# A planner that frees buffers later, first means from tiles already loaded, and pairs of attention tiles in one bank

## The chip, the cores and the metric

The kernel runs on one core of a Trainium2 chip. The metric is device microseconds of one execution, from the median of several runs. Before the change it is 660.25 us (three runs, 660.16 to 660.63). The engines are PE (TensorE: matmuls, with weight loads shown as PEld), ACT (ScalarE), DVE (VectorE), POOL (GpSimd) and SP, which only issues the DMAs here.

## What is computed

Three steps in float32, on q, k, v of 2 x 8 x 768 x 64 (batch, heads, tokens, head size):

```
k_sum = max of k over blocks of 32 tokens;  v_sum = mean of v over blocks of 32 tokens
scores = [ q k^T / 8 where |i - j| < 16, else -1e9 ;  q k_sum^T / 8 + log 32 ]
x = softmax(scores) [ v ; v_sum ]                         # 24 blocks beside the window
x = x / rms(x) * g;  x = (silu(x Wg) * (x Wv)) Wo         # 512 -> 1536 -> 512
out = elu(x Win) Wout                                     # 512 -> 2048 -> 512, 1536 tokens
```

The weights come in as 64-bit floats and are turned into 32-bit ones on the chip.

## The kernel before, in words

**Tiles and stages.** The attention works on 24 tiles of 64 tokens (12 for each batch), all heads of a tile together. A tile needs a copy of the keys of its window and of the 24 block maxima (`copy_keys`), a `scores` group, the softmax on DVE, ACT and POOL, a transpose of the weights (`turn_e`, copied out by `copy_e` to a buffer `ats`) and `apply_v`, 8 matmuls whose outputs are 64 partitions high and which multiply them with the values in one of four buffers `va0` to `va3`: 96 rows of v, loaded for this tile by `load_v`, and below them 24 rows of block means. `copy_x` brings the result into `xT`, the input of the networks for 512 tokens.

The block means are made on PE: `load_vtok` brings 256 tokens of v at a time, 2 tokens to a partition, `mean_v` multiplies them with the constant `blocks` in sets of four matmuls, each 32 partitions high, three calls of two sets for each batch. `place_v` and `repeat_v` put the means into the four `va` buffers.

Tokens are then taken in three blocks of 512. The first network runs in 12 chunks of 128 hidden features per block (`project` twice, gate, `down`), the second in 16 chunks per block: `project` into a PSUM bank `ph`, `elu_a` (exponential, ACT), `elu_b` and `elu_c` (DVE; `elu_c` is the last that reads `ph`), `act_a` and `act_b` that split the result into a high and a low part, and `down`. Both parts of weights and inputs are multiplied, three matmuls of 512 columns for each product. The two parts of a weight are made by `split_a` (a cast, ACT) and `split_b` (a subtraction, DVE) into one of four buffers of the pool `ws`. The attention of the second and third block is woven into the first network of the block before.

**What sets the order.** The class `Order` holds every operation with its engines, its cost in us, a due time, and what it reads and writes. `issue` (L74) plays a schedule forward: an engine that is free takes, of the operations that are ready and for which buffers are free, the one with the least due time; the instructions are then written out in the order in which they were taken, so each engine's order is fixed, and on the chip semaphores alone decide when each starts. A result is ready for another engine 0.2 us after PE's end and 0.13 after any other's (`hop`, L71). A buffer goes back to its pool when the last operation that uses it is popped from a heap of events (L176, L188 to L195). A heap entry is (time, number, kind); entries that only wake the planner, for an operation becoming ready, carry the number -1. `pick` (L124) gives a new tile the first free one of the tags that it may have; for `ph` these are the four banks m0, m1, t0, t1. The due times are written in the `add_...` functions and moved by the table `SHIFT`, by operation and by stretch of due time (`EDGES`). The queue of SP is planned in the same way, and it is the order of the DMAs.

## Time and profile before

| what | value |
|---|---|
| median of the runs | 660.25 us |
| the profiled execution's own time | 660.16 us |
| its span, first to last instruction | 658.0 us |
| PE busy | 644.2 us, 98% |
| DVE / ACT / POOL busy | 455.3 / 360.9 / 70.4 us |
| DMA: bytes moved | 53.42 MB |

Times below are from the start of the span. A busy share counts an engine as busy as long as one of its instructions runs; matmuls overlap, so their starts, not their durations, tell how fast PE goes. In a row of the timeline the number after the start is from the first start to the last end of the merged group, and xN is how many instructions it holds; a float32 matmul of the attention is recorded as two.

### The profile page before, as it was taken

The page shows a single profiled execution, that of the slowest core. Times are in us where ns is not written, and L with a number is a line of the kernel's source. Part 1 is how long each engine was busy: PE and PEld are TensorE (multiplying, and loading weights), DVE is VectorE, ACT ScalarE, POOL GpSimd, SP SyncE. Part 2 cuts the span into 40 slices and gives each one's busy share as a digit, 9 for nine tenths or more (in the row PEclk, how much of TensorE's full clock was granted, in tenths as well). Part 3 has the DMA queues.
Part 4 walks back from the last instruction along what each step waited for, and adds up shares of the span by engine and source line. Part 5 has one row for each costly group of instructions (what it writes and reads, how often), then busy time and mean ns, then how long its engine had stood idle before and what let it go on. Part 6 is the DMA issues. An engine that isn't in the chain of part 4 may idle for free.

```text
span 658.0 us, 9324 instructions
## 1 busy us (share of the span) xinstructions
PE 644.2 (98%) x3424; PEld 525.1 (80%) x3424; DVE 455.3 (69%) x842; ACT 360.9 (55%) x805; POOL 70.4 (11%) x130
## 2 busy tenths in 40 slices
PE   6999998999999999999999999999999999999997
PEld 4888887887888888888888888887787777877776
DVE  6789778857745557489999984655665555755554
ACT  4889768775766664355555553444444334534441
POOL 5741133233000030000000000000000000000000
PEclk9999999999999999999999999999999999999999
DMA  9986995721003000015565300000010000100001
GB/s 224 251 200 197 294 290 170 233 75 45 13 21 130 0 1 1 0 33 188 177 190 185 125 0 1 0 1 0 1 65 0 1 0 1 64 1 1 0 1 64
DMA packets 76957, 53.42 MB, mean 81 GB/s; under 512 B 45168, under 2 KB 71792, under 8 KB 76912
## 3 DMA queue, kind: packets, MB, share of 16 engines
q1 hardware_dynamic: 76912, 52.83, 28.6%
q8 instruction: 27, 0.44, 0.3%
q14 instruction: 18, 0.15, 0.1%
HBM read 49.68 MB, written 3.15 MB: 80 GB/s over the span
## 4 chain that ended last, share of the span: by engine, by line
PE 90%; DVE 4%; ACT 3%; POOL 1%; DMA 1%; SPq 1%; issue 1%; ACTq 0%; POOLq 0%
PE acc L888 34%; PE ph L820 21%; PE pg L820 14%; PE s L613 2%; PE pv L663 2%; PE pv_3c L820 1%; PE pv_7c L820 1%; PE pv_8c L820 1%; PE pv_2c L820 1%; PE pv_11c L820 1%; PE pv_6c L820 1%; PE pv_9c L820 1%; PE at L652 1%; PE pv_1c L820 1%; PE pv_10c L820 1%; PE pv_4c L820 1%
## 5 line engine op out<-in xcount | busy, mean ns | idle before, releaser
L820 PE MATMUL ph<-xb,ws_i 128*128 128x512 f32 x576 | 141.7, 394 | 0.0
L888 PE MATMUL acc<-ws_p,act 128*128 128x512 f32 x576 | 138.3, 389 | 0.0
L820 PEld LDWEIGHTS ph<-xb,ws_i 128*128 128x128 f32 x576 | 105.9, 188 | 30.3 <-issue 9.0
L888 PEld LDWEIGHTS acc<-ws_p,act 128*128 128x128 f32 x576 | 108.1, 188 | 22.5
L888 PE MATMUL acc<-act,ws_o 128*128 128x512 f32 x432 | 107.7, 394 | 0.0
L820 PE MATMUL pg<-x,ws_g 128*128 128x512 f32 (+1 forms) x432 | 105.7, 389 | 0.0
L888 PEld LDWEIGHTS acc<-act,ws_o 128*128 128x128 f32 x432 | 79.8, 188 | 16.6 <-issue 0.2
L820 PEld LDWEIGHTS pg<-x,ws_g 128*128 128x128 f32 x432 | 78.1, 188 | 15.9 <-issue 0.2
L299 DVE TENSOR_TENSOR ws_p<-raw_p,ws_p 128x512 fp32r<-128x512 f32 x48 | 33.2, 691 | 74.1 <-ACT ws_p L288 74.1
L288 ACT CAST ws_p<-raw_p 128x512 fp32r<-128x512 f32 x48 | 29.8, 622 | 89.9 <-PE ph L820 87.8
L288 ACT CAST act<-ex 128x512 fp32r<-128x512 f32 x48 | 29.7, 619 | 49.6 <-DVE ex L868 49.6
L875 DVE TENSOR_TENSOR act<-ex,act 128x512 fp32r<-128x512 f32 x48 | 33.2, 692 | 25.1 <-ACT act L288 24.4
L299 DVE TENSOR_TENSOR ws_g<-raw_g,ws_g 128x512 fp32r<-128x512 f32 x35 | 24.6, 704 | 19.0 <-ACT ws_g L288 18.9
L299 DVE TENSOR_TENSOR ws_i<-raw_i,ws_i 128x512 fp32r<-128x512 f32 x48 | 32.9, 685 | 6.9 <-ACT ws_i L288 6.9
L288 ACT CAST ws_i<-raw_i 128x512 fp32r<-128x512 f32 x48 | 29.8, 620 | 13.9 <-PE ph L820 8.3
L288 ACT CAST ws_o<-raw_o 128x512 fp32r<-128x512 f32 x36 | 22.3, 619 | 23.1 <-PE pg L820 7.8
L868 DVE SCALAR_TENSOR_TENSOR ex<-ph,ex 128x512 f32<-128x512 f32 x48 | 33.1, 690 | 1.4
L288 ACT CAST ws_g<-raw_g 128x512 fp32r<-128x512 f32 x35 | 21.6, 617 | 20.4 <-PE pg L820 13.8
L288 ACT CAST ws_v<-raw_v 128x512 fp32r<-128x512 f32 x35 | 21.7, 619 | 20.2 <-PE acc L888 7.4
L853 DVE SCALAR_TENSOR_TENSOR th<-th,pg 128x512 f32<-128x512 f32 x36 | 24.6, 684 | 6.6 <-ACT th L849 6.4
L860 ACT ACTIVATE ex<-ph 128x512 f32<-128x512 f32 x48 | 28.5, 594 | 0.0
L875 DVE TENSOR_TENSOR act<-th,act 128x512 fp32r<-128x512 f32 x36 | 25.1, 696 | 4.7 <-ACT act L288 4.4
(209 smaller groups left out, 947.7 us busy)
## 6 DMA issues: line engine op xcount, KB each, us to landing
st_i<-in_moe_w_in SPq DMA_DIRECT2D x16, 512.0 KB, 3.8
st_p<-in_moe_w_out SPq DMA_DIRECT2D x16, 512.0 KB, 3.3
st_g<-in_moe_w_gate SPq DMA_DIRECT2D x12, 512.0 KB, 5.2
st_v<-in_moe_w_val SPq DMA_DIRECT2D x12, 512.0 KB, 5.1
st_o<-in_moe_w_out SPq DMA_DIRECT2D x12, 512.0 KB, 4.5
va<-in_v SPq DMA_DIRECT2D x20, 192.0 KB, 5.1
kr<-in_k SPq DMA_DIRECT2D x12, 256.0 KB, 4.9
qr<-in_q SPq DMA_DIRECT2D x12, 256.0 KB, 5.3
```

The source lines that it names most:

```text
L288: nc.scalar.copy(out=out, in_=in_)
L299: (nc.gpsimd if eng == POOL else nc.vector).tensor_sub(out, a, b)
L613: nc.tensor.matmul(pq[:, pr, :], qb[:, t % 2, pr].rearrange("p h c -> p (h c)"), ka[:, pr, :], start=not pre, stop=not pre or pr == NP - 1)
L652: nc.tensor.transpose(pt[:NK, pr, :], T[f"e{b}_{t}"][:, pr, :], ident)
L663: nc.tensor.matmul(pv[64 * h:64 * h + 64, pr, :], va[:NK, 2 * pr + h, :], at[:, pr, QT * h:QT * h + QT], start=True, stop=True)
L820: nc.tensor.matmul(pt[:, i], wt[:, a, kk * P:(kk + 1) * P], xt[:, c, kk, i], start=(kk == 0 and n == 0), stop=(kk == KM - 1 and n == 2))
L853: nc.vector.scalar_tensor_tensor(th, th, 1.0, T[f"pg{b}_{c}"], op0=ALU.add, op1=ALU.mult)
L860: nc.scalar.activation(out=new("t2", f"ex{b}_{c}", [P, TB]), in_=T[f"ph{b}_{c}"], func=AF.Exp)
L868: nc.vector.scalar_tensor_tensor(ex, T[f"ph{b}_{c}"], 0.0, ex, op0=ALU.max, op1=ALU.add)
L875: nc.vector.tensor_sub(t[:, 1], T[src], t[:, 0].bitcast(F32))
L888: nc.tensor.matmul(acc, lhsT, rhs, start=(first and n == 0), stop=(last and n == 2))
```

## The change

- In the planner, a buffer comes free 0.2 us after the end of PE's operation, or 0.13 after another engine's. Entering and leaving the operations with short outputs (`TILED`) now costs 0.2 and 0.13 of PE. Some costs and `DMA_DONE` are changed.
- Batch 0's block means: the blocks of the tokens from 256 on come from loads of 4 tokens to a partition (two DMAs of four heads each, 512 KB); those of the tokens before are made by `mean_own` from the `va` buffers of tiles 0 to 3, which are loaded earlier for it. Batch 1 has a 4-token load pair and a 2-token load pair.
- From tile 8 on two tiles are applied by one `apply_v2` into one bank, and copied out by one `copy_x2`.
- All due times and the table `SHIFT` are new.

```diff
-LIGHT = {"mean_v": 0.7, "apply_v": 0.65}
+LIGHT = {"mean_v": 0.7, "mean_own": 0.7, "apply_v": 0.65, "apply_v2": 0.65}
+TILED = ("mean_v", "mean_own", "apply_v", "apply_v2")
+DRAIN_IN, DRAIN_OUT = 0.2, 0.13
...
-    DMA_START, DMA_DONE = 1.3, 1.2
+    DMA_START, DMA_DONE = 1.3, 1.7
...
-                    end = busy[engine] = self.pe_end(now, cost, LIGHT.get(ops[best][3].__name__, 1.0), ticks) if engine == "PE" else now + cost
+                    if engine == "PE":
+                        name = ops[best][3].__name__
+                        start = now
+                        if (name in TILED) != tiled:
+                            tiled = not tiled
+                            start += DRAIN_IN if tiled else DRAIN_OUT
+                        end = self.pe_end(start, cost, LIGHT.get(name, 1.0), ticks)
+                    else:
+                        end = now + cost
+                    busy[engine] = end
                 if shared(best, engine):
                     port = end
-                heapq.heappush(events, (end, best, 1))
+                heapq.heappush(events, (end + (0.2 if engine == "PE" else 0.13), best, 1))
...
-    blocks = const.tile([P, 2 * NB], F32, name="blocks")
...
+    def selector(name, cols, at, n, rows, base):
+        t = const.tile([P, cols], F32, name=name)
+        nc.gpsimd.memset(t, 0.0)
+        x = t[:, at:at + n]
+        nc.gpsimd.memset(x, 1.0 / BLOCK)
+        nc.gpsimd.affine_select(
+            out=x, in_=x, pattern=[[-rows, n]], compare_op=ALU.is_ge, fill=0.0, base=-base, channel_multiplier=1)
+        nc.gpsimd.affine_select(
+            out=x, in_=x, pattern=[[rows, n]], compare_op=ALU.is_ge, fill=0.0, base=base + rows - 1, channel_multiplier=-1)
+        return t
+    MT = 4
+    sel = {4: selector("sel4", 32, 8, 16, 8, 0), 2: selector("sel2", 32, 0, 8, 16, 0)}
+    own = selector("own", 2 * MT + 30, 2 * MT - 2, 2, BLOCK, W0)
...
+    def load_vtok(b, R, g):
+        hs = slice(4 * g, 4 * g + 4)
+        src = v[b, hs, KB:, :] if R == 4 else v[b, hs, :KB, :]
+        nc.sync.dma_start(out=T[f"vtok{b}_{R}"][:, hs, :R], in_=src.rearrange("h (p r) d -> p h r d", r=R))
+    def mean_v(b, R, first, last, tag):
+        pt = new(tag, f"vp{b}", [P, 2, D]) if first else T[f"vp{b}"]
+        for r in range(R):
             for g in range(4):
                 nc.tensor.matmul(
-                    pt[32 * g:32 * g + 32], blocks[:, NB - 8 - 8 * j:NB + 24 - 8 * j],
...
+                    pt[32 * g:32 * g + 32], sel[R], T[f"vtok{b}_{R}"][:, 2 * g:2 * g + 2, r, :],
+                    start=first and r == 0, stop=last and r == R - 1)
+    def mean_own(t):
+        pt = T["vp0"]
+        for g in range(4):
+            nc.tensor.matmul(
+                pt[32 * g:32 * g + 32], own[:NL, 2 * MT - 2 - 2 * t:2 * MT + 30 - 2 * t],
+                va_bufs[t][:NL, 2 * g:2 * g + 2, :], start=False, stop=t == MT - 1)
...
+        for n, R in enumerate((4, 2) if b else (4,)):
+            vt = f"vtok{b}_{R}"
+            add("-", 0.0, load, take, "xf", vt, [P, H, 4, D], w=[vt], new=[("xf", vt)])
+            for g in range(2):
+                add("SP", 1.75 if R == 4 else 1.0, load + 0.1 * n, load_vtok, b, R, g, r=[vt], w=[f"{vt}#{g}"])
+            add(PE, 0.29 * R, due + 0.5 * n, mean_v, b, R, n == 0, n == 1, tag,
+                r=[f"{vt}#0", f"{vt}#1"], w=[vp], new=[] if n else [(tag, vp)])
...
+        else:
+            for t in range(MT):
+                add_window(0, t, load + 0.5 + 0.1 * t)
+                add(PE, 0.25, due + 0.5 + 0.1 * t, mean_own, t, r=[f"va{t}#a"], w=[vp])
...
+    def apply_v2(b, t, tag):
+        pv = new(tag, f"pv{b}_{t}", [P, NP, 2, QT])
+        for n in range(2):
+            va, at = va_bufs[(b * NQ + t + n) % VA], T[f"ats{b}_{t + n}"]
+            for pr in range(NP):
+                for h in range(2):
+                    nc.tensor.matmul(
+                        pv[64 * h:64 * h + 64, pr, n, :], va[:NK, 2 * pr + h, :], at[:, pr, QT * h:QT * h + QT],
+                        start=True, stop=True)
...
-        add("SP", 0.9, due - 3, load_v, b, t, w=[va + "#a"])
+        if i >= MT:
+            add_window(b, t, due - 3)
...
+        elif t % 2:
+            both = [f"{b}_{t - 1}", n]
+            bufs = [f"va{(i - 1) % VA}", va]
+            add(PE, 1.2, due + 6.3, apply_v2, b, t - 1, tags, r=[f"ats{x}" for x in both] + [x + y for x in bufs for y in ("#a", "#s")],
+                w=[f"pv{both[0]}"], new=[(tags, f"pv{both[0]}")])
+            add({ACT: 0.48}, 0, due + 7.3, copy_x2, b, t - 1, r=[f"pv{both[0]}", f"xT{blk}"],
+                w=[f"xT{blk}#t{off // QT - 1}", f"xT{blk}#t{off // QT}"])
...
-LOOK, URGENT = -0.3, 5
-A0, A_GAP, LATER = 11.8, 1.775, 0.0
-PRE_0, PRE, VS0, MEAN = 0, 8, 4.5, 9.0
-T0, LEAD = 27.5, 8.0
-TILE8, GAP_1, GAP_2 = 3.0, 9.4, 10.2
+TOFF = (3.0, -2.5, -0.5, 0.5, 0.5, -1.5, 0.5, 4.5)
+LOOK, URGENT = -0.9, -80
+A0, A_GAP, LATER = 10.8, 1.975, -0.5
+PRE_0, PRE, VS0, MEAN = 0, 8, 6.0, 8.5
+T0, LEAD = 28.0, 12.0
+TILE8, GAP_1, GAP_2 = 1.0, 7.5, 14.2
...
-K0, QL, VA, PM = 2.1, (1.4, 5.0, 9.5, 11.5), 4, 3
+K0, QL, VA, PM = 4.8, (-1.6, 6.0, 12.0, 9.0), 4, 3
...
-    ('copy_v', 9): 1, ('copy_x', 9): -1, ('elu_a', 9): -6, ('elu_b', 9): 2, ('elu_c', 9): 12, ('exps', 9): 10,
...
+    ('copy_acc', 9): -8, ('copy_k', 9): 1, ('copy_out', 9): 1, ('copy_q', 9): 1, ('copy_v', 9): 7,
+    ('copy_x', 9): -10, ('copy_x2', 9): 0.5, ('diagonal', 9): 9, ('elu_a', 9): 1.5, ('elu_b', 9): 1,
+    ('elu_c', 9): 12, ('gate_a', 9): 2, ('gate_b', 9): 5.5, ('guard', 9): 21, ('invert', 9): -1,
...
-LEN_A, LEN_1, LEN_2 = 8.575, 7.55, 6.15
+LEN_A, LEN_1, LEN_2 = 8.375, 7.45, 5.05
```

The rest of the table `SHIFT` (all of it is replaced) is left out here.

## Rows read from the trace of the kernel before

**Rows 1.** The page's first part: busy time, share of the span, instructions
```profile
PE 644.2 (98%) x3424; PEld 525.1 (80%) x3424; DVE 455.3 (69%) x842; ACT 360.9 (55%) x805; POOL 70.4 (11%) x130
```

**Rows 2.** Waits of PE: us in total, times, longest us
```profile
PE kt L474 <- DMA kr<-in_k: 5.5, 4, 4.4
...
PE slice(0, 512, None)_2098 L762 <- DVE dg1slice(0, 512, None)l L756: 0.2, 1, 0.2
```

**Rows 3.** Waits of the weight loads, 440 to 645 us, the only row
```profile
PEld ph L820 <- issue: 9.0, 28, 0.3
```

**Rows 4.** Timeline of all engines, second network: start, us, instructions, idle before
```profile
444.61 3.00 PE L820 MATMUL ph<-xb,ws_i 128*128 128x512 f32 x12
...
447.45 2.88 PE L888 MATMUL acc<-ws_p,act 128*128 128x512 f32 x12
447.70 0.62 ACT L288 CAST ws_p<-raw_p 128x512 fp32r<-128x512 f32 x1 [2.01 <-PE ph L820]
448.23 0.59 ACT L860 ACTIVATE ex<-ph 128x512 f32<-128x512 f32 x1
448.36 0.69 DVE L299 TENSOR_TENSOR ws_p<-raw_p,ws_p 128x512 fp32r<-128x512 f32 x1 [1.86 <-ACT ws_p L288]
...
449.42 0.69 DVE L868 SCALAR_TENSOR_TENSOR ex<-ph,ex 128x512 f32<-128x512 f32 x1
...
450.22 2.61 PEld L820 LDWEIGHTS ph<-xb,ws_i 128*128 128x128 f32 x12 [0.32 <-issue]
450.25 3.01 PE L820 MATMUL ph<-xb,ws_i 128*128 128x512 f32 x12
```

**Rows 5.** Timeline of PE in the second network, 398 to 413 us
```profile
401.00 2.88 PE L820 MATMUL ph<-xb,ws_i 128*128 128x512 f32 x12
...
411.88 1.30 PE L820 MATMUL ph<-xb,ws_i 128*128 128x512 f32 x5
```

**Rows 6.** Timeline of all engines in that stretch
```profile
411.66 2.68 PEld L820 LDWEIGHTS ph<-xb,ws_i 128*128 128x128 f32 x12
...
412.49 0.69 DVE L868 SCALAR_TENSOR_TENSOR ex<-ph,ex 128x512 f32<-128x512 f32 x1
```

**Rows 7.** Timeline of PE in the first network, 60 to 76 us
```profile
62.84 1.15 PE L663 MATMUL pv<-ats,va 120*64 120x64 f32 x32
63.93 3.06 PE L888 MATMUL acc<-act,ws_o 128*128 128x512 f32 x12
66.82 1.52 PE L820 MATMUL pg<-x,ws_g 128*128 128x512 f32 x6
...
70.78 1.64 PE L820 MATMUL pv_2c<-x,ws_v 128*128 128x512 f32 x6
72.35 0.69 PE L663 MATMUL pv<-ats,va 120*64 120x64 f32 x16
72.96 3.02 PE L820 MATMUL pg<-x,ws_g 128*128 128x512 f32 x12
75.82 0.39 PE L820 MATMUL pv_3c<-x,ws_v 128*128 128x512 f32 x1
```

**Rows 8.** Timeline of PE, 78 to 84 us: six matmuls between two transposes
```profile
80.26 1.64 PE L820 MATMUL pv_3c<-x,ws_v 128*128 128x512 f32 x6
81.73 0.60 PE L652 MATMUL at<-ident,e 128*120 128x128 f32 x4
```

**Rows 9.** Timeline of PE, 93 to 108 us: two calls of `mean_v` together
```profile
95.55 1.08 PE L524 MATMUL vp<-vtok,blocks 128*32 128x128 f32 x32
96.56 1.67 PE L888 MATMUL acc<-act,ws_o 128*128 128x512 f32 x6
```

**Rows 10.** Timeline of SP's DMA issues, first 20 us
```profile
8.69 3.22 SPq L515 DMA_DIRECT2D vtok<-in_v  x3
...
16.44 4.12 SPq L575 DMA_DIRECT2D va<-in_v  x3
```

**Rows 11.** Timeline of POOL, first 24 us
```profile
12.26 0.28 POOL L581 TENSOR_SCALAR ka<-ksum 128x96 f32<-128x96 f32 x1 [4.22 <-DVE ksum L483]
```

More of the change, by code (lines that the diff above doesn't have):

```diff
@@ L113, in issue @@
         ticks = {}
+        tiled = False
         def offer(i):
@@ L669, in copy_x, with add_window @@
         copy(eng, T[f"xT{blk}"][:, :, off:off + QT], T[f"pv{b}_{t}"])
+    def add_window(b, t, due):
+        lo, hi, _ = window(t)
+        va = f"va{(b * NQ + t) % VA}"
+        if hi - lo < NL:
+            add(POOL, 0.46, due - 3, zero_v, b, t, w=[va + "#a"])
+        add("SP", 0.95, due, load_v, b, t, w=[va + "#a"])
     def add_tile(b, t, due, tags):
@@ L703, in add_tile @@
         add(ANY if b * NQ + t < FLEX else {ACT: 0.48}, 0, due + 5.7, copy_e, b, t, r=[f"at{n}"], w=[f"ats{n}"], new=[("ats", f"ats{n}")])
-        add(PE, 0.63, due + 6.3, apply_v, b, t, tags, r=[f"ats{n}", va + "#a", va + "#s"], w=[f"pv{n}"],
-            new=[(tags, f"pv{n}")])
         blk, off = divmod(b * S + t * QT, TB)
@@ L708, in add_tile @@
             add("-", 0.0, due + 4, take, "xf", f"xT{blk}", [P, KM, TB], w=[f"xT{blk}"], new=[("xf", f"xT{blk}")])
-        add({ACT: 0.27, DVE: 0.33} if b * NQ + t < FLEX else {ACT: 0.27}, 0, due + 7.3, copy_x, b, t, r=[f"pv{n}", f"xT{blk}"],
-            w=[f"xT{blk}#t{off // QT}"])
+        if i < TPB:
+            add(PE, 0.61, due + 6.3, apply_v, b, t, tags, r=[f"ats{n}", va + "#a", va + "#s"], w=[f"pv{n}"],
+                new=[(tags, f"pv{n}")])
+            add({ACT: 0.27, DVE: 0.33}, 0, due + 7.3, copy_x, b, t, r=[f"pv{n}", f"xT{blk}"],
+                w=[f"xT{blk}#t{off // QT}"])
+        elif t % 2:
[5 more added lines that the diff above has]
+                w=[f"xT{blk}#t{off // QT - 1}", f"xT{blk}#t{off // QT}"])
     def square(blk, cs, i):
@@ new lines @@
+    ('place_v', 3): 5, ('project', 3): 6, ('project_f32', 3): 17.5, ('repeat_v', 3): -1, ('root', 3): -16,
+    ('row_max', 3): 0.5, ('scale_x', 3): 3, ('scores', 3): -8, ('split_a', 3): -7.5, ('split_b', 3): -23,
+    ('spread', 3): -4.5, ('square', 3): 5.5, ('store', 3): -19.5, ('sum_square', 3): 4, ('take', 3): -8,
+    ('turn_e', 3): 1, ('turn_k', 3): 1, ('x_hi', 3): -4.5, ('zero_v', 3): -1, ('act_a', 4): 3,
+    ('act_b', 4): 8, ('add_mask', 4): -7, ('apply_v', 4): -8, ('apply_v2', 4): -1, ('convert_a', 4): -0.5,
@@ new lines @@
+    ('row_max', 8): 1, ('scale_x', 8): -8.5, ('scores', 8): 4, ('split_a', 8): -1, ('split_b', 8): -5.5,
+    ('store', 8): -0.5, ('sum_square', 8): -1, ('take', 8): 2, ('turn_e', 8): -0.5, ('turn_k', 8): -24,
+    ('zero_v', 8): -1, ('act_a', 9): 13, ('add_mask', 9): 17, ('add_square', 9): 4, ('apply_v', 9): -2.5,
+    ('convert_a', 9): -0.5, ('convert_b', 9): 20, ('convert_c', 9): 8, ('convert_d', 9): -8.5,
+    ('copy_acc', 9): -8, ('copy_k', 9): 1, ('copy_out', 9): 1, ('copy_q', 9): 1, ('copy_v', 9): 7,
```

210 lines of the change are left out of this document (103 added, 107 removed).

## The prediction

> **What bounds the kernel now.** I read the busy shares first: PE is busy for 644.2 of 658.0 us [rows 1]. Nothing off PE can therefore be worth more than it gives PE, and the time falls in two ways only: PE has less to issue, or it stands still less. So I asked for PE's waits next, and then for the stretches in which its matmuls follow each other more slowly than elsewhere, which a busy share hides.
>
> The waits of PE that the profile names come to 9.4 us in eight rows, of which the first and the last stand in [rows 2]: 5.5 are for four of the first k loads, which nothing in this change brings earlier (the six k loads and the first q still open SP's queue, in that order), and 3.9 are the seven others.
>
> The waits of the weight loads show one more place [rows 3]: 28 times in the second network's stage, before a `ph` group, 9.0 us in all, with no releaser named. The timeline says what it is [rows 4]. A `ph` group ends at 447.45. Two things become possible on ACT: `split_a` of a later weight (its buffer in the pool `ws` is free) and `elu_a` of this `ph`. `split_a` goes first (447.70), `elu_a` at 448.23, DVE does `split_b` (448.36) before it comes to `elu_c`, the last reader of `ph`, which starts at 449.42 and ends at 450.11. The next `ph` group's first weight load stands at 450.22, although PE had nothing else before it: it waited for the PSUM bank that `elu_c` was reading. Chunks here take 450.25 - 444.61 = 5.64 us. In the stretch before, two chunks take 411.88 - 401.00 = 10.88, or 5.44 each [rows 5]; there the `ph` group at 411.88 starts before `elu_c` of the one before has even begun (412.49, [rows 6]), so it has another bank. One stall costs 0.20 us of PE, and there are 28: 5.6 us.
>
> **The change part by part.**
>
> *The planner frees late what is used again.* Before, a buffer was free in the plan at the moment `end` of its last user, while a reader of a result came 0.2 (after PE) or 0.13 later. So in the plan ACT was idle at `end`, could take `split_a` 0.2 before `elu_a` was ready, and did; that is the order in rows 4. After, the buffer is free at `end + 0.2` and `elu_a` is ready at `end + 0.2`: the same number. The heap holds the two as (time, -1, 0) and (time, number, 1), the reader's comes out first, and ACT, if idle, takes `elu_a` before the split has a buffer, whatever the due times of the two. Everything in the chain then moves up: `elu_a` would start where `split_a` did, at 447.70, 0.53 earlier than in rows 4; `split_b` (0.69 long) follows instead of preceding. So `elu_c` ends at least 0.53 before 450.11, at about 449.58 or sooner. Without a stall the next `ph` matmul would stand at 447.45 + 2.72 = 450.17 and its weight load 0.22 before, at 449.95 (2.72 is half of 5.44; 0.22 is 411.88 - 411.66, [rows 5, 6]). That is 0.37 us of room, so the stall goes. Term: -5.6. The ends: 0 if the order on ACT stays; more than -5.6 can't come from here. The split that is moved back is for a weight whose turn comes only after the next two groups, over 5 us later, so nothing waits for it.
>
> *Two tiles in one application.* Every `apply_v` that stands alone costs PE more than its own matmuls. Alone [rows 7]: the six matmuls before it take 72.35 - 70.78 = 1.57, against 81.73 - 80.26 = 1.47 for six that also follow a transpose but precede no `pv` [rows 8], so 0.10; its own 72.96 - 72.35 = 0.61; the twelve after it 75.82 - 72.96 = 2.86 against 2.72, so 0.14: 0.85, and two of them 1.70. Side by side, as two already stand at 62.84: 0.10, then 63.93 - 62.84 = 1.09, then 66.82 - 63.93 = 2.89, so 0.17: 1.36. A pair saves 0.34. There are 16 tiles from the ninth on, eight pairs, one of which is a pair already: 7 x 0.34 = 2.4. The ends are 0.13 (2 x 0.61 - 1.09 alone, nothing of the neighbours) and 0.34 each, -0.9 to -2.4; I take -2.4, since rows 7 show just this arrangement. The one copy of a pair in place of two is on ACT and can't be what PE waits for, as the pair's output is needed only when the next 512 tokens are normalised. What the pairing can cost is that the first tile of a pair holds its `ats` and its `va` until the second is ready; the tiles are 7.5 to 14 us apart in the due times, so the planner has the time.
>
> *The first means.* One set of four `mean_v` matmuls costs (96.56 - 95.55) / 4 = 0.25 us [rows 9]. Batch 0 had six sets in three runs, and gets four sets of the 4-token loads and four of `mean_own`: eight, two more, so +0.5 before what the runs' edges cost. In one run instead of three, about 0.2 of that comes back (two edges of 0.10 as above); in five runs 0.4 is added. So +0.3 to +0.9, and I take +0.5. Batch 1 keeps six sets: 0. The Trainium skill, *TensorEngine Tiling (Array Packing)*, Key Properties, says that a change of the tiling mode drains the engine, and not only entering or leaving tiling. Means (32 columns) and applications (64) are two modes there, while the new planner counts them as one class; by that rule a mean put next to an application saves nothing, and the term would be at its upper end, +0.9, and the sum 0.4 higher. No row here has the two side by side.
>
> *Loads.* Batch 0's v is loaded in 2 x 512 KB in place of 3, and the first four tiles' `va` (about 192 KB each), which were loaded anyway, come earlier. SP issued three `vtok` loads in 3.22 us and three `va` loads in 4.12 [rows 10], and the loads of q for tiles 4 to 7 now stand behind four `va` in place of one or none. 0.5 MB less against 0.6 MB moved ahead leaves q's later loads about where they were, and the matmuls of the first four tiles lie beside them: I take 0, with ends of -1.1 (one `vtok` issue less, 3.22 / 3) and +4.1 (three `va` issues more, and nothing beside them). What waits behind those loads is the turn of q on PE, and behind it the scores. The two extra selector tiles are eight small POOL instructions before the masks; at 0.28 each, the row nearest [rows 11], 2.2 us, and POOL stood idle for 4.22 there before the first `ksum` copy. Cost 0; with that cover gone, 2.2.
>
> *The refit.* All due times move, so each of the seven waits of 3.9 us may go and others may come. Delays nearer the trace should leave fewer: I take -1.0, with ends of -3.9 (all gone) and +3.9 (as much again).
>
> **The sum.** 660.16 (the profiled execution; the median of the runs shown is 660.25, so nothing is to be added) - 5.6 - 2.4 + 0.5 + 0 - 1.0 = 651.7 us.
>
> **The rivals.**
> *The bank is still late.* The order on ACT at that moment holds only if ACT is idle when `ph` ends and the planner's bank choice is unchanged; its DVE costs are still short of the trace (0.6 for an `elu_c` that ends after 0.69), so the plan may again take the first bank just before it is free. For it: the choice still goes to the first free tag. Against it: 0.37 us of room above. Then only pairs, means and refit count: 660.16 - 2.4 + 0.5 - 1.0 = 657.3.
> *A stall that grows: slower.* The same place with another order: if DVE has one more instruction ahead of `elu_c` (`elu_c` got a due time 12 later, and splits are due before it), it ends up to 0.69 later (the length of such an instruction in rows 4) and a chunk stalls 0.20 + 0.69. On 28 chunks that is 28 x 0.69 = 19.3 us more: 660.16 + 19.3 - 2.4 + 0.5 - 1.0 = 676.6. It decides from 0.15 us more per chunk on: (2.4 + 1.0 - 0.5 + 1.3) / 28, what the rest gains and the bound for no change given below. Against it: that late due time stood in the plan before too, and what stands ahead needs a free `ws` buffer, which now comes after the readers.
> *A start that is later.* The means wait for the fourth `va`, and the second half of q stands behind them. If PE is idle for the 4.1 us above: 655.8. For it: PE has little slack in that stretch, since its only long waits there are those for k. Against it: four tiles' scores, turns and means are in hand by then.
> *The stages before the second network do nothing.* Pairs at their weak end (-0.9), no wait fewer, means at +0.9, with the bank freed: 660.16 - 5.6 - 0.9 + 0.9 = 654.6.
>
> **How the numbers follow.** Bank freed, with pairs: 0.70, from 648.0 (waits all gone, 651.7 - 2.9; means at +0.3; half of the 1.1 of the loads) to 656.6 (3.9 us of waits more than now in place of 1.0 less: 651.7 + 4.9). Still late: 0.16. Later start or weak ends: 0.07. Slower: 0.07. The range reaches from 648.0 to 657.6, which takes in the second case's time too. A change below 0.2%, 1.3 us, is what a measurement of this kernel can't tell from none. Faster by more: 0.70 + 0.15 + 0.05 = 0.90; within: 0.03; slower: 0.07.
>
> **What would show it.** Right: no idle time of the weight loads before `ph`, or a few rows of it; `elu_a` ahead of the split of `ws` on ACT in the second network; chunks at 5.44 us throughout; `pv` in groups of 32 with about 1.09 between their start and the next. Wrong: chunks still at 5.64, `ph` weight loads idle 28 times or more, or new waits of PE beside those for k that come to more than 3.9 us.

## The result and the profile after

The changed kernel takes 654.46 us (median of 4 runs, 653.42 to 656.62) against 660.33 (4 runs, 660.16 to 660.63): ratio 0.9915, 95% interval 0.9888 to 0.9941. A second set of runs of the same kernel, beside others, gave 654.79 (6 runs, 653.25 to 655.36; ratio 0.990, 0.9886 to 0.9915). The forecast was 651.7, its range 648.0 to 657.6: the time is inside, but 2.8 to 3.1 us above the forecast. The profiled execution is the 653.42, with a span of 651.6, 6.4 less than before.

The first part of the page, beside [rows 1]: PE is 6.1 us less busy.

```profile
PE 638.1 (98%) x3440; PEld 529.5 (81%) x3440; DVE 460.4 (71%) x841; ACT 361.6 (55%) x798; POOL 68.8 (11%) x138
```

The waits of PE after, in the columns of [rows 2]: 4.5 for k (5.5 before), and ten others that come to 4.1 us where there were seven with 3.9. The longest of the ten names `va`, but L607 is the zeroing of a buffer on POOL and not a load.

```profile
PE kt L495 <- DMA kr<-in_k: 4.5, 2, 4.4
PE s L649 <- POOL va L607: 0.8, 1, 0.8
PE acc L955 <- DVE act L942: 0.5, 1, 0.5
...
PE pg L887 <- DVE th L920: 0.2, 1, 0.2
```

The weight loads have no wait left in the second network's stage, where [rows 3] had 28. The timeline of all engines there, in the columns of [rows 4] (L927 is `elu_a`, L935 `elu_c`, L303 a `split_a` or another cast):

```profile
439.67 2.88 PE L887 MATMUL ph<-xb,ws_i 128*128 128x512 f32 x12
...
445.11 2.88 PE L887 MATMUL ph<-xb,ws_i 128*128 128x512 f32 x12
...
447.82 2.88 PE L955 MATMUL acc<-ws_p,act 128*128 128x512 f32 x12
448.02 0.60 ACT L927 ACTIVATE ex<-ph 128x512 f32<-128x512 f32 x1 [2.94 <-PE ph L887]
448.52 0.61 ACT L303 CAST ws_i<-raw_i 128x512 fp32r<-128x512 f32 x1
...
449.12 0.69 DVE L935 SCALAR_TENSOR_TENSOR ex<-ph,ex 128x512 f32<-128x512 f32 x1
449.38 0.62 ACT L303 CAST ws_p<-raw_p 128x512 fp32r<-128x512 f32 x1 [0.25 <-PE acc L955]
...
450.32 0.19 PEld L887 LDWEIGHTS ph<-xb,ws_i 128*128 128x128 f32 x1
```

`elu_a` now starts as the `ph` group ends and both splits follow it; `elu_c` ends at 449.12 + 0.69 = 449.81, and the next weight load, at 450.32, has 0.51 us of room. A chunk is 445.11 - 439.67 = 5.44 us.

To see where the 6.4 us lie I compare the start of the n-th 512- or 256-column matmul of the two networks (2448 of them) in the two traces. From the 800th on the two kernels do the same work in nearly the same order, so the difference there is time won or lost. At the 1200th, shortly before the second network's stage begins, the kernel after is 0.85 us ahead; at the last one 6.47. So 5.62 us were won inside the second network, and only 0.85 in everything ahead of it, where the forecast had 2.4 - 0.5 + 1.0 = 2.9.

Ahead of the 800th the orders differ, and two traces can be compared only where both have issued the same work. Before and after have done so, but for the 16 matmuls of the two added sets of means, at the 91st of these matmuls (70.78 and 74.22 us): there the kernel after is 3.44 us behind. At the 499th (194.98 and 195.48) it is 0.50 behind, at the 781st (270.44 and 269.52) 0.92 ahead. So the 0.85 is a loss of 3.44 us at the start and 4.36 won back from 70 to 270 us.

A pair (L710) beside its neighbours on PE, in the columns of [rows 7]: it takes 63.66 - 62.58 = 1.08, and all eight pairs take that long.

```profile
62.58 1.15 PE L710 MATMUL pv<-ats,va 120*64 120x64 f32 x32
63.66 1.66 PE L887 MATMUL pg<-x,ws_g 128*128 128x512 f32 x6
65.15 1.53 PE L955 MATMUL acc<-act,ws_o 128*128 128x512 f32 x6
```

The start is later. PE in the kernel before:

```profile
13.24 2.01 PE L613 MATMUL s<-ka,qbd 128*128 128x120 f32 x16
...
18.37 0.64 PE L524 MATMUL vp<-vtok,blocks 128*32 128x128 f32 x16
...
21.15 0.69 PE L663 MATMUL pv<-ats,va 120*64 120x64 f32 x16
```

and after:

```profile
14.05 0.66 PE L483 MATMUL qt<-ident,qr 128*128 128x128 f32 x4 [0.50 <-DVE qbd L311]
14.55 1.94 PE L649 MATMUL s<-ka,qbd 128*128 128x120 f32 x16
...
17.66 1.08 PE L549 MATMUL vp<-vtok,sel 128*32 128x128 f32 x32
...
21.37 1.08 PE L556 MATMUL vp<-va,own 96*32 96x128 f32 x32
22.39 0.38 PE L638 MATMUL s<-mask_b,ident_b 128*128 128x480 bf16 x1
...
24.55 0.69 PE L699 MATMUL pv<-ats,va 120*64 120x64 f32 x16
```

The first scores come 1.31 us later and the first application 3.40. All the means stand between the two in both kernels. The application needs the rows that `place_v` copies from them to `va` on DVE; these copies before and then after:

```profile
19.08 1.20 DVE L290 COPY va<-vp 24x128 f32<-24x128 f32 x4 [0.61 <-PE vp L524]
```

```profile
22.52 1.20 DVE L305 COPY va<-vp 24x128 f32<-24x128 f32 x4 [0.38 <-PE vp L556]
```

The last matmul of the means starts at 18.74 before and at 22.18 after, and the first application 2.4 us behind it in both. After, PE has more to do between the first scores and that last matmul: eight more matmuls of scores, a transpose and 16 of means. It does not wait for a `va` there, as the last of the four landed at 19.07.

One cause of the later scores is a load. The first two loads of q, issued at the same times in both kernels (6.3 and 7.5), take longer to land. Their rows among the DMA issues, with the KB of each and the median us to landing, before and then after:

```profile
qr<-in_q SPq DMA_DIRECT2D x2, 256.0 KB, 4.3
```

```profile
qr<-in_q SPq DMA_DIRECT2D x2, 256.0 KB, 5.1
```

The first landed at 10.79 before and at 11.42 after, the second at 11.68 and 12.57, and the first turn of q starts 0.13 to 0.14 behind its load (10.92 and 11.56).

### The profile page after: what moved, and what is told of

Read it like the earlier page. It is cut to its first block, busy times and chain, and to the rows that moved or that the text cites. A ratio compares the mean times of both kernels' runs of the same rounds, so it can differ in the third digit from the quotient of the medians.

```text
span 651.6 us, 9384 instructions
## 1 busy us (share of the span) xinstructions
PE 638.1 (98%) x3440; PEld 529.5 (81%) x3440; DVE 460.4 (71%) x841; ACT 361.6 (55%) x798; POOL 68.8 (11%) x138
## 4 chain that ended last, share of the span: by engine, by line
PE 89%; ACT 5%; DVE 2%; DMA 2%; issue 1%; POOL 0%; SPq 0%; DVEq 0%; ACTq 0%; POOLq 0%
PE acc L955 34%; PE ph L887 20%; PE pg L887 13%; PE s L649 3%; ACT e L665 1%; PE pv_8c L887 1%; PE pv_10c L887 1%; PE pv_1c L887 1%; PE pv_11c L887 1%; PE pv_9c L887 1%; PE pv_2c L887 1%; PE pv_7c L887 1%; PE pv_6c L887 1%; PE pv_5c L887 1%; PE at L688 1%; DMA st_o<-in_moe_w_out 1%
## 5 line engine op out<-in xcount | busy, mean ns | idle before, releaser
L887 PE MATMUL ph<-xb,ws_i 128*128 128x512 f32 x576 | 138.0, 389 | 0.0
L887 PEld LDWEIGHTS ph<-xb,ws_i 128*128 128x128 f32 x576 | 108.2, 188 | 22.4
L887 PE MATMUL pg<-x,ws_g 128*128 128x512 f32 (+1 forms) x432 | 104.3, 388 | 0.2 <-DVE th L920 0.2
L927 ACT ACTIVATE ex<-ph 128x512 f32<-128x512 f32 x48 | 28.8, 599 | 104.0 <-PE ph L887 104.0
L931 DVE TENSOR_SCALAR ex<-ex 128x512 f32<-128x512 f32 x48 | 20.5, 428 | 84.9 <-ACT ex L927 84.8
L303 ACT CAST act<-ex 128x512 fp32r<-128x512 f32 x48 | 29.7, 619 | 21.1 <-DVE ex L935 21.1
L303 ACT CAST ws_p<-raw_p 128x512 fp32r<-128x512 f32 x48 | 29.8, 621 | 17.9 <-PE acc L955 17.9
L916 ACT ACTIVATE th<-pg 128x512 f32<-128x512 f32 x36 | 21.5, 597 | 29.0 <-PE pg L887 27.6
L303 ACT CAST ws_v<-raw_v 128x512 fp32r<-128x512 f32 x35 | 21.6, 617 | 23.6 <-PE acc L955 9.2
L935 DVE SCALAR_TENSOR_TENSOR ex<-ph,ex 128x512 f32<-128x512 f32 x48 | 33.2, 691 | 1.5
L303 ACT CAST ws_i<-raw_i 128x512 fp32r<-128x512 f32 x48 | 29.5, 614 | 3.0 <-PE acc L955 3.0
L942 DVE TENSOR_TENSOR act<-th,act 128x512 fp32r<-128x512 f32 x36 | 27.9, 778 | 3.8 <-ACT act L303 3.2
L665 ACT ACTIVATE e<-e,nm 128x120 f32<-128x120 f32 x64 | 24.5, 386 | 10.7 <-DVE nm L658 10.7
```

Source lines behind the costliest of these rows:

```text
L303: nc.scalar.copy(out=out, in_=in_)
L665: nc.scalar.activation(out=e[:, pr, :], in_=s[:, pr, :], func=AF.Exp, bias=nm[:, pr:pr + 1], accum_out=ss[:, pr:pr + 1])
L887: nc.tensor.matmul(pt[:, i], wt[:, a, kk * P:(kk + 1) * P], xt[:, c, kk, i], start=(kk == 0 and n == 0), stop=(kk == KM - 1 and n == 2))
L916: nc.scalar.activation(out=new("t2", f"th{b}_{c}", [P, TB]), in_=T[f"pg{b}_{c}"], func=AF.Tanh, scale=0.5)
L927: nc.scalar.activation(out=new("t2", f"ex{b}_{c}", [P, TB]), in_=T[f"ph{b}_{c}"], func=AF.Exp)
L931: nc.vector.tensor_scalar(ex, ex, 1.0, -1.0, op0=ALU.min, op1=ALU.add)
```

## The experiments

The kernels ran in three sets, each beside the kernel before: b_delay to a_single (its median there 660.74), b_both to a_warm (660.75) and a_break to bd_warm (660.96); the first row is from the runs of the result. Medians of different sets are compared only roughly. Each kernel's shift against the trace of the kernel before at the 1200th matmul of the networks, and from there to the last, is given as "ahead of the second network" and "inside it". They were read from one profiled execution each. a_again is the kernel after unchanged, so its two numbers show how far executions of one kernel differ; what it lacks inside (-5.15) it lost between the 1250th and the 1300th matmul, at the passage to the second network, and from there to the end it keeps step with the trace of after.

| kernel | median us (runs) | ratio, 95% interval | ahead | inside |
|---|---|---|---|---|
| after | 654.46 (4) | 0.9888 to 0.9941 | -0.85 | -5.62 |
| b_delay | 655.50 (4) | 0.9908 to 0.9933 | +0.94 | -5.70 |
| b_banks | 655.13 (5) | 0.9908 to 0.9932 | +2.60 | -5.69 |
| a_nodelay | 659.37 (12) | 0.9971 to 0.9993 | +1.19 | -0.27 |
| a_single | 658.01 (6) | 0.9938 to 0.9972 | +3.84 | -5.68 |
| b_both | 654.80 (6) | 0.9885 to 0.9932 | +1.42 | -5.50 |
| b_three | 658.56 (7) | 0.9943 to 0.9974 | +4.89 | -5.52 |
| a_means | 657.12 (6) | 0.9927 to 0.9964 | +2.34 | -5.61 |
| a_warm | 654.01 (5) | 0.9874 to 0.9905 | -1.50 | -5.69 |
| a_break | 657.06 (6) | 0.9918 to 0.9961 | +0.28 | -5.67 |
| a_again | 654.79 (6) | 0.9886 to 0.9915 | +0.62 | -5.15 |
| a_warm8 | 656.00 (6) | 0.9906 to 0.9934 | +0.33 | -5.66 |
| bd_warm | 655.13 (4) | 0.9897 to 0.9927 | +0.41 | -5.63 |

### The stall of the second network: three edits of one place

**b_delay** is the kernel before with one line of the planner changed: what `ph` frees is free 0.2 later in the plan.

```diff
-                heapq.heappush(events, (end, best, 1))
+                heapq.heappush(events, (end + 0.2 * (ops[best][3].__name__ == "project" and ops[best][4][0].startswith("ph")), best, 1))
```

> The kernel before, with one line of the planner changed: the buffers of a project group of the second network come free 0.2 us later in the plan, nothing else. Up to the first ph group every engine's order is that of before; in the second network elu_a now goes ahead of the split on ACT. Theory (the stall is ph's bank, held by an elu_c that came late because a split was ahead of elu_a): the 28 idle times of the ph weight loads go, chunks take 5.44 us in place of 5.64, and the time falls by 28 x 0.20 = 5.6 us to 654.7. Rival (the stall comes from the supply of weights or instructions, and the order on ACT has nothing to do with it): the stalls stay, 660.3, or more, since the splits now come later.

655.50 (0.8 over the theory's 654.7), -5.70 inside the second network, and the 28 waits of [rows 3] gone: inside the stage the theory's number to 0.1 us. With +0.94 ahead of that stage, where not one instruction had moved, it also shows how far the first 350 us of two executions lie apart for no reason of the kernel.

**b_banks** leaves the plan alone and changes only which banks the projection takes in turn, so that every engine keeps its order.

```diff
-            add_project(f"ph{n}", MM + AT, f"ws{b}_i{c}", x, [0], t)
+            add_project(f"ph{n}", (MM[c % 2], AT[c % 2]), f"ws{b}_i{c}", x, [0], t)
```

> The kernel before, with the order of every engine as it was; only the PSUM banks of ph are given by turns (even chunks m0 or t0, odd chunks m1 or t1). The split is still ahead of elu_a. Theory (the wait is for the bank that elu_c still reads): another bank is free, the 28 stalls go although elu_c ends as late as before, and the time falls by 5.6 us to 654.7. Rival (the wait is for the order on ACT or DVE itself, or for a weight buffer): nothing changes, 660.3.

655.13, -5.69 inside. The order on ACT stayed as in [rows 4], split first, and the stall still went:

```profile
446.37 0.69 DVE L868 SCALAR_TENSOR_TENSOR ex<-ph,ex 128x512 f32<-128x512 f32 x1
446.90 2.68 PEld L820 LDWEIGHTS ph<-xb,ws_i 128*128 128x128 f32 x12
...
450.10 0.62 ACT L288 CAST ws_p<-raw_p 128x512 fp32r<-128x512 f32 x1 [1.80 <-PE ph L820]
450.62 0.59 ACT L860 ACTIVATE ex<-ph 128x512 f32<-128x512 f32 x1
```

The weight loads of the next `ph` start at 446.90, before `elu_c` has ended (446.37 + 0.69 = 447.06). So PE waited for the bank, and the late `elu_a` mattered only because `elu_c` gives the bank back.

**a_nodelay** is the kernel after with the delay taken out for this one operation.

```diff
-                heapq.heappush(events, (end + (0.2 if engine == "PE" else 0.13), best, 1))
+                heapq.heappush(events, (end + (0.13 if engine != "PE" else 0.0 if ops[best][3].__name__ == "project" and ops[best][4][0].startswith("ph") else 0.2), best, 1))
```

> The kernel after, with the delay taken away for one operation alone: the buffers of a project group of the second network come free in the plan at its end, as before the change. Up to the second network the order is that of after. Theory: the split goes ahead of elu_a again, the stalls come back wherever the bank is used again after one down group (about 25 to 36 chunks at 0.20 us), and the time rises by 5 to 7 us over the kernel after, to 659.5 to 661.5. Rival (the refitted due times of the second network removed the stall, the delay did not): it stays at 654.5.

659.37, 4.9 more than after, with the gain inside the second network down to 0.27. The weight loads' waits in that stage, the columns of [rows 3]:

```profile
PEld ph L887 <- DVE ex L935: 6.4, 24, 0.5
PEld ph L887 <- ACT act L303: 1.1, 4, 0.3
```

28 again, and now 24 of them name `elu_c` (L935), which [rows 3] showed as "issue" without a releaser. All the refitted due times together don't remove what this one number removes.

### Pairs: two kernels on the price of an edge

An edge here is a change between full-width matmuls and the 64-wide ones of an application. **a_single** applies every tile by itself, with the plan otherwise that of after.

```diff
-        if i < TPB:
+        if True:
...
-            add({ACT: 0.27, DVE: 0.33}, 0, due + 7.3, copy_x, b, t, r=[f"pv{n}", f"xT{blk}"],
+            add({ACT: 0.27, DVE: 0.33} if i < TPB else {ACT: 0.27}, 0, due + 7.3, copy_x, b, t, r=[f"pv{n}", f"xT{blk}"],
```

> The kernel after, with every tile applied and copied out by itself (apply_v, copy_x), as before the change. Theory (an application that stands alone pays 0.34 us more than in a pair): eight pairs come apart, less those that the plan puts side by side: 6 to 8 x 0.34 = 2.0 to 2.7 us more than the kernel after, 656.5 to 657.2. Rival (the edges of such a group are covered, or PE waits there anyway): within 0.7 us of the kernel after, 654.5.

658.01: 3.5 us over after, more than expected. But taking pairs out makes the planner place everything behind them anew, with due times that were fitted to pairs. PE then has a wait ahead of `spread` of the second block's normalisation that after doesn't have:

```profile
150.44 0.47 PE L829 MATMUL slice(0, 512, None)_2075<-dg1slice(0, 512, None)h,ones 128*128 128x512 f32 x1 [1.60 <-DVE dg1slice(0, 512, None)h L823]
```

So the next kernel keeps the plan:

**a_break** puts one small matmul between the two tiles of a pair, and what it writes is overwritten.

```diff
+            if n == 0:
+                nc.tensor.matmul(pv[:, 0, 1, :], ident_b, ident_b[:, :QT], start=True, stop=True)
```

> The kernel after, with one small matmul (128 rows, 128 columns out, 64 columns moved, bf16) put between the two tiles of each pair; what it writes is overwritten by the second tile. The plan and every engine's order stay as they are. Theory: what a pair saves is the change of array shape in the middle, 0.10 us going into the 64-wide matmuls and 0.14 coming out of them, 0.13 less for the second sixteen, so eight pairs cost 8 x 0.37 = 3.0 us more with their small matmul: about +2.5 to +3.5 over the kernel after in the fast half of its runs, and the first sixteen of a group followed by a visible gap. Rival (the 3.5 us that single tiles cost came from a plan re-flowed, not from the edges): +0.2 to +0.6, the small matmuls alone.

The timeline of PE at the first pair, where after had 62.58 to 63.66:

```profile
62.47 0.69 PE L710 MATMUL pv<-ats,va 120*64 120x64 f32 x16
63.08 0.20 PE L714 MATMUL pv<-ident_b 128*128 128x64 bf16 x1
63.22 0.69 PE L710 MATMUL pv<-ats,va 120*64 120x64 f32 x16
63.83 1.66 PE L889 MATMUL pg<-x,ws_g 128*128 128x512 f32 x6
```

A broken pair takes 63.83 - 62.47 = 1.36 in place of 1.08. All eight do (1.365 to 1.367 against 1.080 to 1.082), so 0.284 each and 2.27 for the eight. The medians say 657.06 - 654.79 = 2.27 against the same kernel unbroken on the same chip, though with runs from 654.49 to 658.93 that agreement is luck; the profiled execution, the quickest, ended only 1.07 behind the trace of after, presumably since some of the 0.28 fell on gaps that were there anyway. It is under the 3.0 of the theory: a stretch of 16 takes 0.61 whatever stands next to it, so what a pair saves inside is 2 x 0.615 - 1.08 = 0.15, and the small matmul takes the other 0.14. The neighbours' share, 0.09 going in (six matmuls ahead of a `pv` take 1.56, six others behind a transpose 1.47, [rows 8]) and 0.13 coming out (1.49 against half of 2.72), is not in the broken pair. A real pair saves both: 0.15 + 0.09 + 0.13 = 0.37, close to the 0.34 forecast from [rows 7]. By these rows the rival, edges for nothing, is out; the times alone could not tell, as the eight small matmuls with 0.14 each come to 1.1 by themselves.

### The parts one after another, from before

**b_both** is b_delay with pairs, **b_three** that with the first means and loads of after as well; due times and shifts stay those of before.

```diff
+        elif t % 2:
+            add(PE, 1.2, due + 6.3, apply_v2, b, t - 1, tags, ...)
+            add({ACT: 0.48}, 0, due + 7.3, copy_x2, b, t - 1, ...)
```

> The kernel before with two parts of the change: the one-line delay of b_delay, and tiles from the ninth on applied and copied out in pairs (due times of apply_v and copy_x as they were). Theory (a pair saves 0.34 us, seven pairs are new, the delay is worth what b_delay showed): 655.5 - 2.4 = 653.1, that is 0.988 of before; the kernel after is then no better than these two parts, and the first means with the refit brought nothing or cost something. Rival (the pairing costs elsewhere, since a tile must wait for its partner): 655 or more.

```diff
-        for j in range(NG // 2):
-            add(PE, 0.58, due + 0.5 * j, mean_v, b, j, tag, ...)
+        for n, R in enumerate((4, 2) if b else (4,)):
+            add(PE, 0.29 * R, due + 0.5 * n, mean_v, b, R, n == 0, n == 1, tag, ...)
+            for t in range(MT):
+                add(PE, 0.25, due + 0.5 + 0.1 * t, mean_own, t, r=[f"va{t}#a"], w=[vp])
```

> b_both with the new first means as well: 4-token loads, and mean_own from the first four tiles' va buffers (their loads now stand ahead of the later q loads). The rest of the plan and its due times are those of before. Theory (two more sets of matmuls, +0.5, and later q loads cost PE some idle time in the first 50 us): 0.5 to 3 us over b_both, 653.6 to 656. Rival (0.5 MB less to load makes the start earlier): 1 us or more under b_both.

b_both: 654.80 (652.59 to 658.15), 0.7 under b_delay, where 653.1 was expected, 1.7 lower; its interval overlaps b_delay's. b_three: 658.56, 3.8 worse than b_both, over the upper end of what was expected; its first application is at 23.62 (b_both 21.56), its first two q loads landed at 11.28 and 12.44 (10.61 and 11.50), and it is 2.45 us behind b_both at the first matmul of the networks (50.35 against 47.90), with the same work done but for the 16 matmuls of the added sets. Put into the old plan, the new means alone cost nearly all that pairs and refit could give back.

b_both spread far, and the granted clock goes with it: its three runs with a mean clock of 0.999 or 1.000 took 652.59 to 654.04, the three with 0.994 to 0.997 took 655.56 to 658.15. The profiled execution, one of the latter, shows a place: its new order has PE wait 2.2 us for a `th` of DVE, and then the granted clock falls. The wait, and the stretches around it (columns: stretch, its length, busy time and instructions of PE, PEld, DVE, ACT and POOL, the granted clock, the DMA engines' share, GB/s):

```profile
104.61 2.93 PE L844 MATMUL pg<-x,ws_g 128*128 128x512 f32 x6 [2.19 <-DVE th L877]
```

```profile
95.00:101.00 6.00, 6.00 (x73) 5.06 (x72) 4.05 (x7) 4.55 (x14) 3.80 (x5) 1.00 0.73 189
103.00:105.00 2.00, 0.39 (x1) 0.39 (x2) 2.00 (x4) 0.93 (x4) 1.86 (x3) 0.87 1.23 300
105.00:109.00 4.00, 4.00 (x19) 3.31 (x19) 3.00 (x6) 1.52 (x4) 0.06 (x1) 0.64 0.68 201
109.00:115.00 6.00, 6.00 (x28) 4.93 (x28) 4.22 (x7) 4.41 (x16) 2.19 (x4) 1.00 0.55 197
```

Six matmuls (104.61) that take 1.49 elsewhere take 107.34 - 104.61 = 2.73: the lower of the two levels, 1.2 GHz, for most of 4 us, on top of the wait.

**a_means** goes the other way: after, with batch 0's means made like batch 1's, from six sets of loaded v.

```diff
-        for n, R in enumerate((4, 2) if b else (4,)):
+        for n, R in enumerate((4, 2)):
...
-        else:
-            for t in range(MT):
-                add_window(0, t, load + 0.5 + 0.1 * t)
-                add(PE, 0.25, due + 0.5 + 0.1 * t, mean_own, t, r=[f"va{t}#a"], w=[vp])
```

> The kernel after, with batch 0's means made as those of batch 1 (4-token and 2-token loads of all of v, no mean_own; the first four tiles' loads are due with their tiles). Theory (the new means cost PE 0.3 to 0.9 and give nothing back): the same as the kernel after within 1 us, 653.5 to 655. Rival (the new means make the start earlier): 1 us or more slower than after, 655.5 or more.

657.12: 2.7 worse than after, though the first application came at 22.05 in place of 24.55. The trace is 3.19 behind that of after at the 1200th matmul, but hardly by the means: where both have done the same work, but for the 16 matmuls of the two sets, a_means is 2.0 behind at 82 us, level at 111 and 0.1 behind at 140. At 159 us it is 3.1 behind. In between PE waits twice for DVE at the second block's normalisation, ahead of the sums of squares and of `spread`, where after has no such wait:

```profile
142.42 1.13 PE L789 MATMUL slice(0, 512, None)_1974<-ones,slice(0, 512, None)_1897 128*128 128x128 f32 x8 [1.83 <-DVE e L650]
...
148.74 0.50 PE L824 MATMUL slice(0, 512, None)_2038<-dg1slice(0, 512, None)l,ones 128*128 128x512 f32 x1 [0.82 <-DVE dg1slice(0, 512, None)l L818]
```

So the earlier application gave no lead that lasted to 111 us, and nearly all of the loss came with the order that the planner made behind it, from due times fitted to the other means.

### The clock at the start

In the profile of after the weight loads of the first k turns take 0.71 to 0.72 us for four, and from 14 us on 0.42: the lower level of the clock, and then the upper. In that of before they fall to 0.42 at 8.0 us. The profile's own clock column reads 1.00 from the start in both, so the level is read here from the length of the loads; where the column shows the lower level, in bd_warm from 10 to 12 us (columns as in the stretches of b_both), four loads take 0.71 too:

```profile
10.14 0.71 PEld L474 LDWEIGHTS kt<-ident,kr 128*128 128x128 f32 x4 [0.27 <-issue]
```

```profile
10.00:12.00 2.00, 2.00 (x11) 1.64 (x10) 0.77 (x2) 1.17 (x2) 0.00 (x0) 0.50 1.02 235
```

Three kernels with matmuls on a constant tile ahead of the first k turn test whether that is the lost time: **a_warm** (after, twenty of 128 columns), **a_warm8** (after, eight of 512) and **bd_warm** (b_delay, the same eight). **a_again** is after unchanged beside them.

```diff
+    warm = pools["a3"].tile([P, 4, P], F32, tag="a3", name="warm")
+    for i in range(8):
+        nc.tensor.matmul(warm, ones_r, ones_r.unsqueeze(1).to_broadcast([P, 4, P]), start=True, stop=True)
```

> The kernel after, with 20 matmuls of 128 columns on a constant (their result is not used) on PE before the first k turn, when PE has nothing to do. In the kernel after PE ran at the lower of its two clocks until about 13 us into the span, in the one of before until about 8. Theory (the turns, premasks and first scores at the lower clock cost about 1.3 us, and more in some executions, which is why the kernel after spreads over 3 us): the turns run at the full clock from the start, the time falls by about 1 us to 653.5 and the spread shrinks. Rival (the first stretch waits for the k loads anyway, and the clock there costs nothing): 654.5 as before, same spread.

> The kernel after with eight matmuls of 512 columns on a constant tile (fp32r, into a bank nobody uses yet) ahead of the first turn of k; nothing else moves. Theory (part of the late start is the granted clock, which stood at its lower level for the first 12 to 13 us of the kernel after): PE is loaded from about 1.1 to 4.6 us, the clock rises before the k turns at about 6 us in place of 10 us with the twenty small ones, and the first scores come at 13.3 to 13.9 in place of 14.55: 0.7 to 1.5 us under the kernel after. Rival (the k loads and the DVE sums set the first scores): the first scores stay at 14.0 or later and the gain is 0 to 0.5, as with the twenty small ones.

> The kernel before with the late release of ws and t buffers for the second network's first projection (the one-line edit of b_delay) and the same eight warming matmuls; all tiles single, means as before. b_delay alone gave 655.5, with the clock already up at 7.8 us in its profile. Theory (the stall is worth 5.7 and the clock at the start under 1): 654.5 to 655.3. It would equal the whole change. Rival (the clock at the start costs nothing, or the warming delays the k turns): 655.3 to 656.0.

> The kernel after itself, unchanged, timed beside the others on this chip, as the base for them: 653.4 to 656.6 us, as in its first runs. If its median here is under 653.5, the two microseconds that it missed the forecast by were largely spread from run to run; if it is at 654.5 again, they belong to the kernel.

a_warm gave 654.01, a_warm8 656.00, bd_warm 655.13 (b_delay: 655.50), a_again 654.79. a_warm8 had the upper clock from its first k turn on (0.60 to 0.66 for four, against 1.1), and yet:

```profile
6.82 0.63 PE L495 MATMUL kt<-ident,kr 128*128 128x128 f32 x4 [0.81 <-DMA kr<-in_k]
7.99 0.63 PE L495 MATMUL kt<-ident,kr 128*128 128x128 f32 x4 [0.55 <-DMA kr<-in_k]
9.18 0.63 PE L495 MATMUL kt<-ident,kr 128*128 128x128 f32 x4 [0.56 <-DMA kr<-in_k]
...
14.10 1.94 PE L649 MATMUL s<-ka,qbd 128*128 128x120 f32 x16
```

The k turns still come every 1.2 us, only with waits between them, and the scores start at 14.10. The profile puts these waits down to the k loads, and the landings bear it out: these three landed at 6.68, 7.86 and 9.04, and each turn starts 0.13 to 0.14 behind. The chain from turn to copy to sum can go faster: in a_warm, where the first turns had to stand behind the twenty matmuls while loads came in, turns follow each other every 0.9 us. DVE in that stretch, after:

```profile
10.89 0.69 DVE L504 TENSOR_REDUCE ksum<-kT 128x16 f32<-128x512 f32 x1 [0.52 <-ACT kT L303]
12.09 0.69 DVE L504 TENSOR_REDUCE ksum<-kT 128x16 f32<-128x512 f32 x1 [0.51 <-ACT kT L303]
13.30 0.69 DVE L311 TENSOR_SCALAR qbd<-qt 64x512 f32<-64x512 f32 x1 [0.53 <-ACT qbd L309]
14.75 0.68 DVE L311 TENSOR_SCALAR qbd<-qt 64x512 f32<-64x512 f32 x1 [0.75 <-PE qt L483]
```

Before, the last `ksum` was at 11.49 and both `qbd` followed at 12.21. The second turn of q now waits for the first `qbd` (14.05 in the rows of PE above), which it didn't. Of 1.31 us at the first scores, 0.63 are the later landing of the first q load; the clock can claim what a_warm8 gained, 14.55 - 14.10 = 0.45 (against a_again's trace, where the scores were at 14.81, 0.71); the rest, about 0.2, is this order. In the traces of all kernels with the 4-token loads of v the first q load lands at 11.27 to 11.46, in those without at 10.61 to 10.88. b_three, which adds only the new means and their loads to b_both, has it 0.67 later. So it comes with the new means and their loads, most likely with the v loads themselves, though they stand behind q in the queue; why is not shown.

What the warming won at the start a_warm8 did not keep: it was ahead of a_again's trace by 2.3 us at the 200th matmul of the networks and by 0.3 at the 1200th. One piece of it: PE, being early, had to wait 0.34 us for a weight split on DVE at 141 us. The trace of a_warm kept its lead over that of after, 0.65 us at the 1200th. The theory that the granted clock is the lost time falls: its share at the first scores is 0.45 of 1.31, and a_warm's 654.01 and a_warm8's 656.00 lie on both sides of the kernel unwarmed.

How much the clock can vary between executions of one kernel is plain in a_again. Its first sixteen scores took 3.31 us in place of 1.94, at the lower level:

```profile
14.81 3.31 PE L649 MATMUL s<-ka,qbd 128*128 128x120 f32 x16
```

That is 1.4 of the 1.5 us by which its trace is behind that of after at the 1200th matmul. No kernel here beats the change by more than the intervals allow; a_warm's median is the lowest, 0.45 under after, 0.8 under a_again, and the two were not timed beside each other. Nor is the whole change clear of the one-line edit: bd_warm, with none of the new means, pairs or due times, gave 655.13 (655.00 to 655.69) beside a_again's 654.79 (653.25 to 655.36).

## Why the prediction was right, and where it was not

**The stall (-5.6).** Right in place, mechanism and size: -5.62 in the trace of after, and -5.70, -5.69 and -0.27 where it was removed in two other ways and put back. The step from "no releaser named" to the bank of `elu_c` was an inference from [rows 4 to 6]; b_banks and the releaser in a_nodelay show it. The order on ACT came as forecast, `elu_a` first, and the room before the next weight load was 0.51 us against at least 0.37. Neither rival that lives there came: no stall was left, none grew.

**The pairs (-2.4).** The size was right: 0.37 by the rows of the traces with pairs and singles, 0.34 forecast. a_break bounds it from below on the chip at 0.28 less the small matmul's own time; a_single, 3.5 worse in all, has a new wait of 1.6 us among that and so bounds it only loosely. That seven pairs put the whole 2.4 on the path isn't shown. The 4.36 us that after wins back between 70 and 270 us have room for it: seven pairs by the rows, 2.6, and the wait of 1.7 that is gone come to 4.3.

**The means (+0.5).** Batch 0's stretches were 3 x 0.58 = 1.73 us before and are 2 x 1.014 = 2.03 now: +0.30, the lower end. Batch 1's are 1.447 in one run where they were 1.011 + 0.574 = 1.585: -0.14, forecast as 0. In after that run stands right behind a pair of applications, and takes 1.447 there, as it does behind scores in b_both, and the pair takes its usual 1.08: neither is shorter for standing beside the other. That agrees with the rule of the Trainium skill (*TensorEngine Tiling (Array Packing)*, Key Properties) that a change of mode drains, but this place held only one such edge, so the 0.4 us of the rule's sum did not come. Whether the full-width neighbours of such a place save something isn't shown.

**Loads (0) and the later start.** This is where the forecast failed. Means and loads together were put at +0.5, and by 71 us the kernel after is 3.44 late. Two steps were missing. The forecast looked for a cost of the DMAs only in "q behind four `va`"; the one that came is at the first two q loads, which stand ahead of all of v and land 0.63 and 0.89 later. And it left out order: the first application has to follow the last of the means, and the plan put the second half of them, 1.02 us of PE, behind scores and a transpose that had come after all the means. The last of the means went from 18.74 to 22.18, and the first application with it from 21.15 to 24.55. The rival "a start that is later" had the place, with 655.8, by another cause: PE did not stand idle behind the second half of q. The fourth rival's 654.6 is nearest to the time, and its reasons are wrong: the pairs are not at their weak end, nor the means at their dear one. That the time still fell inside the range is in part luck: a start worse by 2.9 was made up in part by the 1.0 more than forecast that came behind it.

**The refit (-1.0).** Not seen in the waits: 4.1 us in ten for 3.9 in seven; one of 1.7 us went and more short ones came. By the letter one of the prediction's signs of being wrong, waits beside those for k of more than 3.9, is met by 0.2. Between 70 and 270 us pairs and refit together gave 4.36 where 3.4 were forecast, but what the due times alone gave there no run tells. Forecasting a gain from "delays nearer the trace" had nothing behind it.

The sum by what was measured, from places with the same work done: +3.44 up to the 91st matmul, -4.36 from there to the 781st, -5.55 from there to the last, which is the stall with 0.07 lost on the way: -6.47. The medians of the two sets give -5.9 and -6.2 (654.46 - 660.33 and 654.79 - 660.96). What the new means, new loads and refit are worth each stays open: they were fitted together, and every kernel with one of them undone or done alone was worse, by 2.7 to 3.8 us, nearly all of it in a_means and some of it in a_single by waits that the planner's new order brought at 142 to 150 us.

## What to carry to other kernels

A weight load that waits "for issue" at the same place in every iteration is worth a look at the engines' order: the last reader of the bank that it needs may stand behind work nobody is waiting for, and one number in the planner, or another turn of banks, gives all of it back. Forecast an edit that leaves each engine's order alone by its rows, to a few tenths of a microsecond; of an edit after which a planner re-orders a tuned start, take back a few microseconds, whatever the rows promise, and ask first which new operation will stand ahead of the first long chain. Test the worth of an edge by breaking it inside the unchanged plan, not by taking the edit out of it; and before a slower variant is held against an edit, compare its trace at places with the same work done, and see whether one wait elsewhere holds the difference.

## What the runs showed of the hardware

- A granted clock can fall in the midst of the work, not only at its ends: in b_both after PE had waited 2.19 us, in b_banks after 2.26 (the clock 0.55 from 109 to 112 us; the six matmuls of `pg` at 108 took 2.63 in place of 1.49). The length of the wait alone doesn't tell: in b_delay, with the order of b_banks there, a wait of 2.22 us at the same place was followed by 1.00, and so was one of 1.7 in bd_warm.
- Warming the engine didn't always hold the clock: in bd_warm the weight loads of the k turns took 0.42 us for four at 6.8 and 8.0 us, and 0.71 again at 9.2 to 11.0, after waits of about 0.58 between the turns (the clock column shows 0.79 from 8 to 10 us and 0.50 from 10 to 12). In a_warm8, with the same eight matmuls and waits of 0.55 to 0.57, they stayed at 0.42.
- The first two q loads stand ahead of all v loads in SP's queue, and took 5.1 us to land after, with v loaded by 4 tokens to a partition, and 4.3 before, with 2, at 512 KB a load in both. That loads behind them put them off is likely, and not shown by a kernel that changes nothing else.
- Sixteen 64-wide matmuls with no wait behind them took 0.615 to 0.618 us in the traces of before, after, a_single and a_break, beside full ones, scores and a single 64-column matmul; the price of the change of shape shows in the neighbours, 0.09 ahead and 0.13 behind. Not all of the 0.13 need be the shape's: six matmuls between two transposes of full width took 1.47, 0.11 over half of 2.72.
